# A two-layer attention and feed-forward kernel: stage order set anew with GpSimd's measured durations, one copied column less, unread matmuls in planned idle times

## The chip, the cores and the metric

The kernel runs on one core of one Trainium2 chip, as one program. The metric is the device time in microseconds (us). A core has five engines with a queue each: TensorE (PE, matmuls, with the loading of weights shown apart as PEld), VectorE (DVE), ScalarE (ACT), GpSimd (POOL) and SyncE (SP, which here issues nearly all DMAs). Each engine executes its own queue in order, and waits for other engines by semaphores.

## The reference

Four blocks are applied to x (2048 rows of 512), attention, feed-forward, attention, feed-forward, each as x + block(layernorm(x)). All of it is fp32.

```python
# attention, 32 heads of 16, 4 segments of 512 rows; M and z start at 0
for s in range(N):
    logits = einsum("bhqd,bhkd->bhqk", qs, ks) * scale + mask
    a_dot = einsum("bhqk,bhkd->bhqd", softmax(logits), vs)
    num = einsum("bhld,bhde->bhle", phi(qs), M)
    den = einsum("bhld,bhd->bhl", phi(qs), z)[..., None] + 1e-6
    outs.append(g * num / den + (1.0 - g) * a_dot)
    M = M + einsum("bhld,bhle->bhde", phi(ks), vs)
    z = z + einsum("bhld->bhd", phi(ks))
# then the heads are put together and multiplied by wo
# feed-forward, 1792 inner columns
(silu(x @ w_gate) * (x @ w_up)) @ w_down
```

## The kernel before

**Numbers.** An fp32 operand is split into a rounded high part (written by ACT, or by POOL in L492) and a rest (high subtracted again, by DVE or POOL). Three one-pass matmuls, high by high, rest by high and high by rest, take the place of one fp32 matmul.

**Attention.** A layer has 32 units (4 segments, 4 groups of heads, 2 halves). `qk_proj` projects q and k of a group (L295, the helper of all projections), ACT copies the result (L491), POOL splits it (L492, L494), and SP writes it to memory and reads it back in another layout (`load3`, tiles cq and ck, cleared beforehand by POOL in L522 to L525). `mx_units` takes row maxima (PE L558, DVE L564, transposed by PE in L573, then written by an ACT DMA), `at_units` makes the exponentials (PE L609, ACT L615, POOL's causal mask L619), multiplies with v (L636) and normalises on DVE. `mem_read` and `mem_update` (L690, L706, L718) carry the memory M, z. `wo_proj` ends a segment. Layernorm statistics run on DVE and POOL (L367 to L379), and the normalised rows are transposed by PE against the identity matrix `ident` (L387), which DVE and POOL make at the start (L319, L320).

**Feed-forward.** The inner 1792 columns are 7 chunks of 256, the 2048 rows 4 blocks of 512, taken as two pairs (m = 0 and 1). Chunk 0 is computed plainly (`up`, L1017). Chunks 1 to 6 use a scheme with seven products for a pair of row blocks (`strassen`, L1047, sums on DVE in L1060). It needs sums of row blocks, the four T tiles, made once per pair by `make_t` (sums L961, high part on ACT L982, rest on DVE L983), and sums of weight blocks, made for each chunk by `load_s`: two raw loads, four sums on POOL (L900), then high parts on ACT (L913) and rests on POOL (L914). `gate` and `finish` apply silu and the product (L998 to L1004), `down` multiplies with w_down and adds to the residual on DVE (L1091, L1096). `load_d` loads w_down's part, with the rests on POOL (L867).

**The order of the work.** No order is written out by hand. The program first records every operation with an engine, an assumed cost, its dependences and a priority, which is a due time: `at(v)` sets it to a base plus v times a stage length. The constants `PRE` (start of a layer), `OFF` (steps of an attention unit), `EP` (chunk 0), `PAIR`, `STEP`, `WAT`, `TAT`, `FIN` and `WQ1` are such due times. Then `issue` simulates all engines: whenever an engine is free, it takes the operation of lowest due time among those that are ready, and that order is the order of the engine's queue in the program. It also gives out the 8 PSUM banks (tag "ps"). Assumed costs matter only through this order. POOL's are written as numbers at each call of `gp`.

**The copied column.** `pool_turn` (L918) makes POOL copy one column of a tile. Operations that are made to depend on this copy come behind it in POOL's queue, so they start only when that tile has been written. Ahead of a chunk c > 1 the tile is the second one of the chunk before's gated product; ahead of chunk 1 of the second pair it is the T tile TT[2], whose rests DVE writes. The up weights of the chunk, the gate weights of the next one and w_down's part wait for it.

Of the kernel before, what the change touches and what calls it, by code (L numbers as in the profile page):

```python
# [12 lines left out]
OP = mybir.AluOpType  # L13
# [11 lines left out]
NB = 3  # L25
CAP = {'pj': 3, 'plt': 3, 'pmx': 3, 'ppv': 3, 'ff': 6, 'st': 6}
LPW = 3
WOT = ("st", "st", "pj", "pj")
EARLY_AT = (23, 25, 26)
PAIR, STEP, WAT, TAT = 11.852, 7.441, 15.217, (16.363, 16.627)  # L30
T3E = "dve"
FIN = 4.95
WQ1 = -11.849
TA, TF = 15.0, 16.7
OFF = ({'qe': (-8.094, 0.816), 'at': (3.287, 3.306), 'mx': (-0.131, -0.724), 'lf': (1.377, -12.744), 'mr': (-1.477, 8.495), 'mu': (-0.96, 1.713), 'wo': (1.48, 1.471), 'qk': (-3.167, 5.871), 'v': (3.082, -3.254), 'lp': (-0.438, 1.332)},
       {'qe': (-13.863, -20.735), 'at': (1.287, 1.907), 'mx': (0.952, -1.245), 'lf': (-8.163, -17.558), 'mr': (12.428, -6.81), 'mu': (-3.524, 1.251), 'wo': (0.699, 4.133), 'qk': (2.417, 0.184), 'v': (-2.402, 1.541), 'lp': (-15.902, 3.529)})
PRE = {'w1': -7.923, 'w2': -0.782, 'w3': 1.908, 'c': -7.288, 'mb': 12.995, 'lv': 2.037, 'lo': 1.091, 'gate': 1.265, 'v': 1.734, 'dv': 17.818, 'qk1': -29.691, 'mx': -0.352}
EP = {'w': 7.501, 'wn': 13.81, 'ln': -3.176, 'dn': -0.03, 'up': -1.79}
POOL_W = ""
TABLE = 1.28  # L40
DRAIN = {("full", "cols"): 0.097, ("cols", "full"): 0.147}
# [38 lines left out]
class Program:  # L80
# [70 lines left out]
    def issue(self):  # L151
# [102 lines left out]
def infini_swiglu(ctx: ExitStack, tc: tile.TileContext, x, wq, wk, wv, wo, beta, wg, wu, wd, out,  # L254
# [33 lines left out]
    def gp(cost, fn, reads, writes):  # L288
        op("pool", cost, fn, reads, writes)
# [75 lines left out]
    def ln_norm(xt, view, xk, tags, on_act=False):  # L365
        st, mv, rs = sb("bst", [128, 6], ring=4), sb("bmv", [128, 2], ring=4), sb("brs", [128, 2], ring=4)
        dve(512, lambda: nc.vector.bn_stats(out=st.ap, in_=view(xt.ap)), [(xt, xk)], [st])  # L367
        dve(8, lambda: nc.vector.bn_aggr(out=mv.ap, in_=st.ap), [st], [mv])
        gp(0.18, lambda: nc.gpsimd.tensor_scalar_add(mv.ap[:, 1:2], mv.ap[:, 1:2], EPS), [mv], [mv])
        gp(0.46, lambda: nc.gpsimd.tensor_tensor(out=rs.ap[:, 0:1], in0=mv.ap[:, 1:2], in1=mhalf.ap, op=OP.pow),  # L370
           [mv, mhalf], [rs])
        dve(4, lambda: nc.vector.scalar_tensor_tensor(out=rs.ap[:, 1:2], in0=mv.ap[:, 0:1], scalar=-1.0,
                                                      in1=rs.ap[:, 0:1], op0=OP.mult, op1=OP.mult), [mv, rs], [rs])
        xn = sb(tags, [128, 512])
        if on_act:
            act(512, lambda: nc.scalar.activation(xn.ap, view(xt.ap), AF.Identity, scale=rs.ap[:, 0:1],
                                                  bias=rs.ap[:, 1:2]), [(xt, xk), rs], [xn], sbuf=True)
            return xn
        gp(0.75, lambda: nc.gpsimd.tensor_scalar(out=xn.ap, in0=view(xt.ap), scalar1=rs.ap[:, 0:1],  # L379
                                                 scalar2=rs.ap[:, 1:2], op0=OP.mult, op1=OP.add),  # L380
           [(xt, xk), rs], [xn])
        return xn
# [27 lines left out]
    def attention(lay, x_in, x_out, slots, T, hook):  # L410
# [70 lines left out]
        def qk_proj(s, n, nm, tag="pj"):  # L481
            g = GRP.setdefault((s, n), {})
            if "nat" not in NAT:
# [5 lines left out]
                lambda kc: n, lambda kc: None, "b")  # L489
            raw = sb("raw", [128, 512])  # L490
            act(512, lambda: nc.scalar.copy(raw.ap, ps.ap), [ps], [raw])  # L491
            gp(0.59, lambda: nc.gpsimd.tensor_scalar(out=nat.ap[:, a, 0, :], in0=raw.ap, scalar1=1.0, scalar2=0.0,  # L492
                                                     op0=OP.mult, op1=OP.add), [raw], [(nat, (a, 0))])
            gp(1.23, lambda: nc.gpsimd.tensor_sub(nat.ap[:, a, 1, :], raw.ap, nat.ap[:, a, 0, :].bitcast(F32)),  # L494
               [raw, (nat, (a, 0))], [(nat, (a, 1))])
            if (nm == "q" and s > 0) or (nm == "k" and s < NSEG - 1):
                ph = sb(f"phik_{n - 2}" if s == nseg - 1 and n > 1 else f"phi{nm}_{n % 2}", [128, 512])
# [87 lines left out]
        def at_units(u):  # L585
# [16 lines left out]
            def lt(kt, qt):  # L602
                def f():
# [12 lines left out]
                        view().rearrange("p x i c -> p (x i c)"), ps.ap, AF.Exp, scale=SCALE), [ps], [(Pb, key)],  # L616
                        table="exp")
                    if kt == qt:
                        gp(0.593, lambda: nc.gpsimd.affine_select(  # L619
                            out=view()[:, 0], in_=view()[:, 0], pattern=[[0, 4], [1, 128]], compare_op=OP.is_ge,  # L620
                            fill=0.0, base=0, channel_multiplier=-1), [(Pb, key)], [(Pb, key)])
                return f
# [25 lines left out]
            def post():  # L648
# [10 lines left out]
                if h == 1:  # L659
# [14 lines left out]
                    gp(1.23, lambda: nc.gpsimd.tensor_sub(tl.ap[:, n, :], of.ap, th.ap[:, n, :].bitcast(F32)),  # L674
                       [of, (th, n)], [(tl, n)])

            units = [lt(0, q) for q in range(4)] + [lt(1, q) for q in (1, 2, 3)]
# [169 lines left out]
    def ffn(base, x_in, x_out, slots, T):  # L847
# [40 lines left out]
        def load_s(c, nm, after=()):  # L888
# [8 lines left out]
            S1, S2, S3, S4 = [lambda i=i, o=o: m[i].ap[:, o] for i, o in ((0, 1), (0, 0), (1, 0), (1, 1))]  # L897

            def ew(f, out, x, y, reads, w_):
                gp(0.65, lambda: getattr(nc.gpsimd, f)(out(), x(), y()), reads, [w_])  # L900
# [5 lines left out]
            for wt, o0, o1, src, read in ((a, 0, 1, lambda: v0()[:, :, 0:128].rearrange("p k (o f) -> p o k f", o=1), r0),  # L906
                                          (a, 1, 3, lambda: m[0].ap, m[0]),
                                          (b, 0, 2, lambda: v1().rearrange("p k (o f) -> p o k f", o=2), r1),
                                          (b, 2, 4, lambda: m[1].ap, m[1])):
                n = 256 * (o1 - o0)  # L910
                hi = lambda wt=wt, o0=o0, o1=o1: wt.ap[:, o0:o1, 0]
                lo = lambda wt=wt, o0=o0, o1=o1: wt.ap[:, o0:o1, 1]
                act(n, lambda hi=hi, src=src: nc.scalar.copy(hi(), src()), [read], [(wt, (o0, 0))], sbuf=True)  # L913
                gp(n / 400, lambda hi=hi, lo=lo, src=src: nc.gpsimd.tensor_sub(lo(), src(), hi().bitcast(F32)),  # L914
                   [read, (wt, (o0, 0))], [(wt, (o0, 1))])
                P.ops[-1].deps |= set(after)

# [211 lines left out]
        for m in range(2):  # L1129
# [24 lines left out]
            for c in range(1, NF):  # L1154
# [93 lines left out]
```

## Time and profile before

| | us |
|---|---|
| median of 3 runs | 1881.71 |
| lowest and highest | 1880.82, 1883.06 |
| the profiled execution | 1878.99 |
| its span, first to last instruction | 1877.2 |
| its mean granted TensorE clock | 0.995 |

In rows of the profile, L12 is line 12 of the kernel before. A row of the view by windows gives the stretch, its length, the busy time and the number of instructions of PE, PEld, DVE, ACT and POOL, the share of TensorE's full clock that was granted (PEclk), the DMA share and GB/s. A row of the view of waits gives who waited for whom, the total in us, how often, and the longest. A row of the timeline gives start and duration in us, engine, line, operation, output and inputs, how many instructions were merged, and in brackets the engine's idle time before it and what ended it. A row of a group gives the count, busy time in us and mean duration in ns.

### The profile page before, as it was taken

The page shows a single profiled execution, that of the slowest core. Times are in us where ns is not written, and L with a number is a line of the kernel's source. Part 1 is how long each engine was busy: PE and PEld are TensorE (multiplying, and loading weights), DVE is VectorE, ACT ScalarE, POOL GpSimd, SP SyncE. Part 2 cuts the span into 40 slices and gives each one's busy share as a digit, 9 for nine tenths or more (in the row PEclk, how much of TensorE's full clock was granted, in tenths as well). Part 3 has the DMA queues.
Part 4 walks back from the last instruction along what each step waited for, and adds up shares of the span by engine and source line. Part 5 has one row for each costly group of instructions (what it writes and reads, how often), then busy time and mean ns, then how long its engine had stood idle before and what let it go on. Part 6 is the DMA issues. An engine that isn't in the chain of part 4 may idle for free.

```text
span 1877.2 us, 33021 instructions
## 1 busy us (share of the span) xinstructions
PE 1825.3 (97%) x11360; PEld 1450.6 (77%) x11360; DVE 1407.5 (75%) x3834; ACT 873.1 (47%) x1629; POOL 918.9 (49%) x1186
## 2 busy tenths in 40 slices
PE   7999999999999999999989999999999999999999
PEld 5787787877778887788867877778777788878887
DVE  6878788778876678766776777787898766796656
ACT  4565564555533432433345655556454433333432
POOL 6344444444655654647533444444446647445551
PEclk9999999999999999999999999999999999999999
DMA  7535444464232132111373353455642311312121
GB/s 236 148 102 147 135 133 144 144 214 119 74 119 61 46 91 89 52 50 57 114 217 101 106 163 115 130 167 140 188 124 74 123 51 56 94 64 57 44 58 45
DMA packets 126967, 206.14 MB, mean 110 GB/s; under 512 B 14160, under 2 KB 52048, under 8 KB 126800
## 3 DMA queue, kind: packets, MB, share of 16 engines
q1 hardware_dynamic: 124752, 203.49, 36.7%
q8 instruction: 91, 1.49, 0.3%
q10 hardware_dynamic: 2048, 0.53, 0.1%
q14 instruction: 76, 0.62, 0.1%
HBM read 136.34 MB, written 67.11 MB: 108 GB/s over the span
## 4 chain that ended last, share of the span: by engine, by line
PE 48%; DVE 7%; issue 2%; DMA 2%; POOL 1%; ACT 1%; SPq 0%; DVEq 0%; POOLq 0%; ACTq 0%
PE ps L1047 18%; PE ps L1091 10%; PE ps L295 7%; PE ps L636 3%; PE ps L558 3%; PE ps L609 3%; DVE junk L564 2%; DMA s<-nm 1%; PE ps L1017 1%; DVE tt L961 1%; DVE s L983 1%; DVE s L1096 1%; PE ps L387 1%; DVE mx L564 0%; DVE of L961 0%
## 5 line engine op out<-in xcount | busy, mean ns | idle before, releaser
L1047 PE MATMUL ps<-s,s 128*128 128x512 f32 x2016 | 547.3, 396 | 9.5 <-ACT s L982 4.6
L295 PE MATMUL ps<-s,s 128*128 128x512 f32 x1536 | 526.2, 407 | 2.7 <-ACT s L451 1.2
L564 DVE CUSTOM_DVE_ANT_0 junk<-ps,amask 128x128 bf16<-128x128 f32 (+3 forms) x1024 | 433.5, 484 | 46.5 <-PE ps L558 45.1
L1047 PEld LDWEIGHTS ps<-s,s 128*128 128x128 f32 x2016 | 376.7, 188 | 106.0 <-ACT s L982 6.7
L1091 PE MATMUL ps<-s,vt 128*128 128x512 f32 x1296 | 378.0, 397 | 2.2 <-ACT vt L1003 2.2
L295 PEld LDWEIGHTS ps<-s,s 128*128 128x128 f32 x1536 | 287.2, 191 | 51.6 <-issue 6.1
L615 ACT ACTIVATE s<-ps 128x512 f32<-128x512 f32 x448 | 253.9, 609 | 108.5 <-PE ps L609 97.2
L1091 PEld LDWEIGHTS ps<-s,vt 128*128 128x128 f32 x1296 | 245.2, 189 | 58.6 <-ACT vt L1003 2.6
L558 PE MATMUL ps<-ck,s 127*128 127x256 f32 (+2 forms) x1024 | 276.6, 334 | 5.7 <-DMA ck<-scrk 4.9
L609 PE MATMUL ps<-s,ck 128*128 128x256 f32 x1280 | 250.6, 287 | 6.4 <-DMA s<-nm 4.5
L609 PEld LDWEIGHTS ps<-s,ck 128*128 128x128 f32 x1280 | 221.3, 189 | 38.3 <-issue 4.9
L1096 DVE TENSOR_TENSOR s<-s,ps 128x512 f32<-128x512 f32 x224 | 150.1, 683 | 92.0 <-PE ps L1091 91.7
L619 POOL TENSOR_SCALAR_AFFINE_SELECT s<-s 128x512 f32<-128x512 f32 x192 | 126.8, 663 | 171.9 <-ACT s L615 166.6
L558 PEld LDWEIGHTS ps<-ck,s 127*128 127x128 f32 x1024 | 177.6, 189 | 28.8 <-issue 6.4
L914 POOL TENSOR_TENSOR s<-mem,s 128x512 fp32r<-128x512 f32 x96 | 130.7, 1362 | 0.0
L492 POOL TENSOR_SCALAR s<-raw 128x512 fp32r<-128x512 f32 x64 | 45.4, 709 | 173.9 <-ACT raw L491 163.6
L1017 PE MATMUL ps<-s,s 128*128 128x512 f32 x384 | 123.9, 400 | 0.9 <-ACT s L391 0.9
L921 POOL COPY turn<-vt 128x1 f32<-128x1 f32 x20 | 3.7, 186 | 235.6 <-DVE vt L1004 235.6
L636 PE MATMUL ps<-s,vt 128*32 128x384 f32 (+3 forms) x1536 | 115.7, 419 | 0.1
L636 PEld LDWEIGHTS ps<-s,vt 128*32 128x32 f32 x1536 | 43.3, 109 | 64.1 <-issue 46.2
L615 ACT ACTIVATE pc<-ps 128x512 f32<-128x512 f32 x128 | 78.7, 615 | 19.9 <-PE ps L609 19.3
L494 POOL TENSOR_TENSOR s<-raw,s 128x512 fp32r<-128x512 f32 x64 | 84.3, 1317 | 4.3
(172 smaller groups left out, 2585.3 us busy)
## 6 DMA issues: line engine op xcount, KB each, us to landing
s<-scrq SPq DMA_DIRECT2D x128, 192.0 KB, 3.5
ck<-scrk SPq DMA_DIRECT2D x128, 192.0 KB, 4.5
scrq<-s SPq DMA_DIRECT2D x32, 512.0 KB, 3.6
scrk<-s SPq DMA_DIRECT2D x32, 512.0 KB, 3.3
scrq<-s SPq DMA_DIRECT2D x32, 256.0 KB, 3.2
scrk<-s SPq DMA_DIRECT2D x32, 256.0 KB, 2.5
s<-xmid SPq DMA_DIRECT2D x32, 256.0 KB, 5.2
xin<-xmid SPq DMA_DIRECT2D x32, 256.0 KB, 2.7
```

Source lines behind the costliest of these rows:

```text
L295: pe(n, passes, lambda: nc.tensor.matmul(view(ps.ap), lhsT=av(a.ap), rhs=bv(b.ap), start=start, stop=stop), [(a, rk[0]), (b, rk[1])], [ps])
L558: nc.tensor.matmul(ps.ap[:, a * 256:a * 256 + nk], lhsT=cq.ap[0:127, 2 * j + p, qt * 128:(qt + 1) * 128], rhs=ck.ap[0:127, p, 0:nk], start ...
L564: dve(w, lambda a=a, qt=qt, w=w, ps=ps, junk=junks[qt % 2]: nc.vector.tensor_tensor_reduce(out=junk.ap[:, :w], in0=ps.ap[:, a * 256:a * 25 ...
L609: nc.tensor.matmul(ps.ap[:, 256 * p:256 * p + 256], lhsT=ck.ap[:, p, kt * 128:kt * 128 + 128], rhs=cq.ap.rearrange("r (j p) c -> r p j c", ...
L615: act(512, lambda: nc.scalar.activation(view().rearrange("p x i c -> p (x i c)"), ps.ap, AF.Exp, scale=SCALE), [ps], [(Pb, key)], table="exp")
L619: gp(0.593, lambda: nc.gpsimd.affine_select(out=view()[:, 0], in_=view()[:, 0], pattern=[[0, 4], [1, 128]], compare_op=OP.is_ge, fill=0.0, ...
L636: nc.tensor.matmul(ps.ap[32 * i:32 * i + 32, qt * 128:(qt + k) * 128], lhsT=vt.ap[:, kt, VW * hd:VW * hd + 32], rhs=view(k=k)[:, :, idx], ...
L914: gp(n / 400, lambda hi=hi, lo=lo, src=src: nc.gpsimd.tensor_sub(lo(), src(), hi().bitcast(F32)), [read, (wt, (o0, 0))], [(wt, (o0, 1))])
L1017: pe(512, 1, lambda i=i, j=j, kc=kc, x=x, ps=ps, wt=wt: nc.tensor.matmul(ps.ap, lhsT=wt.ap[:, i, kc, cs], rhs=XT[b][j].ap[:, :, kc], start ...
L1047: pe(512, 1, lambda i=i, kc=kc, x=x, buf=buf, view=view: nc.tensor.matmul(ps.ap, lhsT=w.ap[:, o, i, kc], rhs=view(buf.ap, kc), start=(x == 0),
L1091: pe(512, 1, lambda i=i, j=j, fi=fi, x=x, ps=ps, wt=wt, cs=cs: nc.tensor.matmul(ps.ap, lhsT=ht.ap[:, 0:2048].rearrange("p (f a c) -> p f a ...
L1096: dve(512, lambda ps=ps, t=t: nc.vector.tensor_add(xb.ap[:, t, :], xb.ap[:, t, :], ps.ap), [ps, (xb, t)], [(xb, t)])
```

## The change

Three things change, and no matmul of the computation is added or removed.

1. Assumed costs of POOL's operations are raised, and all due times are set anew.
2. The copied column ahead of chunk 1 of the second pair is left out (before, only the first pair had none).
3. `issue` puts runs of unread matmuls into PE's queue. Where the simulated PE is idle for over 0.8 us, and a PSUM bank is free since before that idle time, it emits as many matmuls of 128 columns as fit at 0.215 us each, less 0.35 us, at most 16. They multiply half of `ident` by itself in fp32, into the bank that came free last, and nothing reads the result. The simulation itself takes no account of them. For the first run PE counts as idle from 3.5 us on.

```diff
+WARM = (0.8, 0.35, 16)
...
-PAIR, STEP, WAT, TAT = 11.852, 7.441, 15.217, (16.363, 16.627)
+PAIR, STEP, WAT, TAT = 11.353, 1.597, 1.08, (12.624, 17.012)
...
-FIN = 4.95
-WQ1 = -11.849
+FIN = -2.787
+WQ1 = -3.055
...
-PRE = {'w1': -7.923, 'w2': -0.782, 'w3': 1.908, 'c': -7.288, 'mb': 12.995, 'lv': 2.037, 'lo': 1.091, 'gate': 1.265, 'v': 1.734, 'dv': 17.818, 'qk1': -29.691, 'mx': -0.352}
-EP = {'w': 7.501, 'wn': 13.81, 'ln': -3.176, 'dn': -0.03, 'up': -1.79}
+PRE = {'w1': -7.357, 'w2': -1.301, 'w3': 4.634, 'c': 6.066, 'mb': 18.459, 'lv': 4.718, 'lo': -0.662, 'gate': 1.688, 'v': 9.33, 'dv': 18.454, 'qk1': -33.774, 'mx': -8.469}
+EP = {'w': -0.609, 'wn': 14.483, 'ln': -1.109, 'dn': -5.448, 'up': -16.361}
...
-        done, bus, table, mode = 0, 0.0, "exp", "full"
+        done, bus, table, mode, idle = 0, 0.0, "exp", "full", 3.5
...
+            if e == "pe":
+                spare = max([fr for fr in free["ps"] if fr[0] <= idle], default=None)
+                beats = min(WARM[2], int((start - idle - WARM[1]) / 0.215)) if start - idle > WARM[0] else 0
+                if spare and beats:
+                    self.warm(spare[1], beats)
...
+            if e == "pe":
+                idle = t[e]
...
+    def warm(slot, beats):
+
+        t = psum.tile([128, 512], F32, name=f"ps_{slot}", tag=f"ps_{slot}")
+        for _ in range(beats):
+            nc.tensor.matmul(t[:, 0:128], lhsT=ident.ap[0:64], rhs=ident.ap[0:64], start=True, stop=True)
+    P.warm = warm
...
-                elif m == 0:
+                else:
                     turn = []
-                else:
-                    turn = pool_turn(lambda t=TT[2]: t.ap[:, 1, 3, 1, 127:128], (TT[2], (1, 1)))
```

All ten entries of `OFF` change for both layers in the same manner (least those of maxima and exponentials, by at most 1.3 units of 15 us, most those of layernorm, by up to 17.7). POOL's assumed costs change like this:

| operation | line | before, us | after, us |
|---|---|---|---|
| power in layernorm | L370 | 0.46 | 0.60 |
| normalise 512 columns | L379 | 0.75 | 0.85 |
| high part of q, k | L492 | 0.59 | 0.70 |
| rest of q, k; of the attention's output | L494, L674 | 1.23 | 1.32 |
| causal mask | L619 | 0.593 | 0.66 |
| sum of weight blocks | L900 | 0.65 | 0.85 |
| rest of n weight columns | L914 | n / 400 | 0.3 + n / 480 |

More of the change, by code (lines that the diff above doesn't have):

```diff
@@ L369, in ln_norm @@
         gp(0.18, lambda: nc.gpsimd.tensor_scalar_add(mv.ap[:, 1:2], mv.ap[:, 1:2], EPS), [mv], [mv])
-        gp(0.46, lambda: nc.gpsimd.tensor_tensor(out=rs.ap[:, 0:1], in0=mv.ap[:, 1:2], in1=mhalf.ap, op=OP.pow),
+        gp(0.6, lambda: nc.gpsimd.tensor_tensor(out=rs.ap[:, 0:1], in0=mv.ap[:, 1:2], in1=mhalf.ap, op=OP.pow),
            [mv, mhalf], [rs])
@@ L378, in ln_norm @@
             return xn
-        gp(0.75, lambda: nc.gpsimd.tensor_scalar(out=xn.ap, in0=view(xt.ap), scalar1=rs.ap[:, 0:1],
+        gp(0.85, lambda: nc.gpsimd.tensor_scalar(out=xn.ap, in0=view(xt.ap), scalar1=rs.ap[:, 0:1],
                                                  scalar2=rs.ap[:, 1:2], op0=OP.mult, op1=OP.add),
@@ L491, in qk_proj @@
             act(512, lambda: nc.scalar.copy(raw.ap, ps.ap), [ps], [raw])
-            gp(0.59, lambda: nc.gpsimd.tensor_scalar(out=nat.ap[:, a, 0, :], in0=raw.ap, scalar1=1.0, scalar2=0.0,
+            gp(0.70, lambda: nc.gpsimd.tensor_scalar(out=nat.ap[:, a, 0, :], in0=raw.ap, scalar1=1.0, scalar2=0.0,
                                                      op0=OP.mult, op1=OP.add), [raw], [(nat, (a, 0))])
-            gp(1.23, lambda: nc.gpsimd.tensor_sub(nat.ap[:, a, 1, :], raw.ap, nat.ap[:, a, 0, :].bitcast(F32)),
+            gp(1.32, lambda: nc.gpsimd.tensor_sub(nat.ap[:, a, 1, :], raw.ap, nat.ap[:, a, 0, :].bitcast(F32)),
                [raw, (nat, (a, 0))], [(nat, (a, 1))])
@@ L618, in f @@
                     if kt == qt:
-                        gp(0.593, lambda: nc.gpsimd.affine_select(
+                        gp(0.66, lambda: nc.gpsimd.affine_select(
                             out=view()[:, 0], in_=view()[:, 0], pattern=[[0, 4], [1, 128]], compare_op=OP.is_ge,
@@ L673, in post @@
                     act(512, lambda: nc.scalar.copy(th.ap[:, n, :], of.ap), [of], [(th, n)], sbuf=True)
-                    gp(1.23, lambda: nc.gpsimd.tensor_sub(tl.ap[:, n, :], of.ap, th.ap[:, n, :].bitcast(F32)),
+                    gp(1.32, lambda: nc.gpsimd.tensor_sub(tl.ap[:, n, :], of.ap, th.ap[:, n, :].bitcast(F32)),
                        [of, (th, n)], [(tl, n)])
@@ L899, in ew @@
             def ew(f, out, x, y, reads, w_):
-                gp(0.65, lambda: getattr(nc.gpsimd, f)(out(), x(), y()), reads, [w_])
+                gp(0.85, lambda: getattr(nc.gpsimd, f)(out(), x(), y()), reads, [w_])
                 P.ops[-1].deps |= set(after)
@@ L913, in load_s @@
                 act(n, lambda hi=hi, src=src: nc.scalar.copy(hi(), src()), [read], [(wt, (o0, 0))], sbuf=True)
-                gp(n / 400, lambda hi=hi, lo=lo, src=src: nc.gpsimd.tensor_sub(lo(), src(), hi().bitcast(F32)),
+                gp(0.3 + n / 480, lambda hi=hi, lo=lo, src=src: nc.gpsimd.tensor_sub(lo(), src(), hi().bitcast(F32)),
                    [read, (wt, (o0, 0))], [(wt, (o0, 1))])
```

4 lines of the change are left out of this document (2 added, 2 removed).

## The prediction

> **What bounds the kernel now.** I read the page's head first, then the busy times by stage, then what TensorE (PE) waited for, then the timeline where it waited longest.
>
> ```profile
> span 1877.2 us, 33021 instructions
> ...
> PE 1825.3 (97%) x11360; PEld 1450.6 (77%) x11360; DVE 1407.5 (75%) x3834; ACT 873.1 (47%) x1629; POOL 918.9 (49%) x1186
> ```
>
> PE is busy for 1825.3 of 1877.2 us, and the change removes no useful matmul. So a gain has to come out of the 51.9 us in which PE is idle, or out of matmuls that run slowly. By stage:
>
> ```profile
> core 0: us, PE busy (x) PEld busy (x) DVE busy (x) ACT busy (x) POOL busy (x), PEclk, DMA share, GB/s
> 0.00:60.00 60.00, 43.43 (x192) 34.55 (x193) 39.90 (x131) 27.69 (x50) 31.55 (x54) 0.97 0.73 220
> 60.00:440.00 380.00, 377.25 (x3175) 301.16 (x3174) 298.50 (x1141) 215.04 (x425) 165.44 (x249) 1.00 0.49 145
> 440.00:720.00 280.00, 275.74 (x1386) 216.42 (x1386) 213.06 (x420) 117.42 (x211) 157.96 (x187) 1.00 0.27 81
> 720.00:760.00 40.00, 35.71 (x149) 27.89 (x148) 37.41 (x63) 12.94 (x24) 23.10 (x24) 0.91 0.29 92
> 760.00:900.00 140.00, 140.00 (x606) 113.27 (x605) 89.74 (x137) 54.36 (x95) 78.38 (x85) 1.00 0.19 55
> 900.00:1000.00 100.00, 91.84 (x444) 73.77 (x446) 76.37 (x215) 40.27 (x73) 43.12 (x51) 1.00 0.52 156
> 1000.00:1400.00 400.00, 393.46 (x3331) 310.99 (x3323) 311.02 (x1190) 223.64 (x440) 172.30 (x264) 1.00 0.50 141
> 1400.00:1640.00 240.00, 237.66 (x1109) 188.19 (x1108) 175.89 (x291) 100.38 (x176) 138.97 (x161) 1.00 0.26 78
> 1640.00:1700.00 60.00, 56.74 (x245) 44.92 (x244) 51.99 (x79) 22.84 (x40) 28.14 (x28) 0.97 0.21 71
> 1700.00:1877.00 177.00, 173.44 (x748) 139.46 (x746) 113.62 (x174) 58.47 (x101) 79.89 (x88) 1.00 0.16 50
> ```
>
> The chunks of the feed-forward part are full: 760 to 900 has no idle PE and 606 matmuls in 140 us, 0.231 us each. No order is faster there. Idle PE time lies in six places: 16.6 us at the start, 2.8 and 6.5 in the two attention stages (60 to 440, 1000 to 1400), 4.3 in 720 to 760 and 3.3 in 1640 to 1700 (each the change to the second pair of row blocks), 8.2 around the change of layers, and 3.6 at the end. What ended the waits:
>
> ```profile
> PE ps L387 <- ACT xn L376: 9.8, 1, 9.8
> PE ps L558 <- DMA ck<-scrk: 4.9, 4, 2.8
> PE ps L573 <- DVE mx L564: 4.7, 9, 1.7
> PE ps L1047 <- ACT s L982: 4.6, 4, 2.6
> ...
> PE ps L1047 <- POOL s L914: 4.2, 2, 3.1
> PE ps L706 <- DVE phik L501: 3.0, 1, 3.0
> ```
>
> The first wait of 9.8 us and the last 3.6 us no order of matmuls takes away. Beside idle time there are stretches at half clock (column PEclk):
>
> ```profile
> 20.00:40.00 20.00, 16.98 (x68) 12.52 (x67) 10.30 (x19) 7.61 (x13) 12.10 (x20) 0.91 0.90 273
> 740.00:760.00 20.00, 16.15 (x58) 12.11 (x57) 18.27 (x28) 6.25 (x13) 14.99 (x14) 0.83 0.10 26
> 1200.00:1220.00 20.00, 18.50 (x113) 14.13 (x112) 12.59 (x42) 10.93 (x21) 8.16 (x10) 0.91 0.49 139
> 1680.00:1700.00 20.00, 17.59 (x69) 13.69 (x70) 14.24 (x19) 7.99 (x14) 15.27 (x14) 0.91 0.22 67
> ```
>
> They cost 20 x (0.09 + 0.17 + 0.09 + 0.09) = 8.8 us in all, behind waits. So about 51.9 - 9.8 - 3.6 + 8.8 = 47 us is the most that better order and warmth could ever give; a few of them are in reach.
>
> **The copied column.** Only the second pair of row blocks has it ahead of chunk 1, once a layer:
>
> ```profile
> 746.44 1.18 POOL L921 COPY turn<-s 128x1 f32<-128x1 f32 x1 [3.87 <-DVE s L983]
> 751.76 0.73 PE L1047 MATMUL ps<-s,s 128*128 128x512 f32 x1 [3.15 <-POOL s L914]
> 1675.07 0.58 POOL L921 COPY turn<-s 128x1 f32<-128x1 f32 x1 [18.05 <-DVE s L983]
> 1682.15 0.50 PE L1047 MATMUL ps<-s,s 128*128 128x512 f32 x1 [2.56 <-ACT s L982]
> ```
>
> GpSimd (POOL) stands in this copy for 3.87 and 18.05 us until VectorE (DVE) has written the last part of one T tile; behind it in POOL's queue are the sums and splits of chunk 1's up weights, and PE at 751.76 waits 3.15 us for just such a split (L914). Without the copy the four sums (L900) can run at once; the splits still need the old weights' place. In the first layer the copy and its wait leave, so L914 ends several us earlier and the 3.15 us go; next late is the T tile (L982), and it is fed by DVE. There is a price, which DVE's rows before and behind the copy show:
>
> ```profile
> L961 DVE TENSOR_TENSOR tt<-s,s 128x512 f32<-128x512 f32 x4 | 2.6, 681 | 0.0
> ...
> L961 DVE TENSOR_TENSOR of<-of,s 128x512 f32<-128x512 f32 x1 | 1.2, 1219 | 0.0
> ```
>
> While POOL is silent (1660 to 1675) an addition of the T chain takes 0.681 us; beside POOL's sums 1.219, which is 0.54 more. Four sums laid beside the chain delay it by up to 4 x 0.54 = 2.2 us, but the same 2.2 us are then missing behind. First layer: 3.15 us of wait and 20 x 0.17 = 3.4 us of half clock, less 2.2: between -6.6 (all saved) and +2.2; I take -4, since the wait hangs on L914 alone. Second layer: 2.56 us and 1.8 us of half clock hang on the DVE chain itself, which gets no shorter; between -4.4 and +2.2, and I take -1.5.
>
> **The start.** In the second row POOL clears tiles ahead of making ident; the change moves these memsets back in priority.
>
> ```profile
> 0.79 0.95 POOL L522 MEMSET s<- 128x1024 f32 x1 [0.29 <-POOLq L1235]
> ...
> 3.55 0.29 POOL L320 TENSOR_SCALAR_AFFINE_SELECT ident<-ident 128x128 f32<-128x128 f32 x1
> ...
> 28.70 0.45 PE L706 MATMUL ps<-ident,phik 128*128 128x128 f32 x1 [3.02 <-DVE phik L501]
> ...
> L387 PE MATMUL ps<-ident,xn 128*128 128x128 f32 x16 | 3.8, 428 | 9.8 <-ACT xn L376 9.8
> L295 PE MATMUL ps<-s,s 128*128 128x512 f32 x8 | 3.6, 626 | 1.2 <-ACT s L451 1.2
> ...
> L295 PE MATMUL ps<-s,s 128*128 128x512 f32 x30 | 7.8, 406 | 0.0
> ```
>
> The first 8 matmuls of L295 take 3.6 us, 0.45 each, the next 30 take 7.8, 0.26 each: PE starts at half speed. The planned idle time ahead of the first transposes surely asks for a full run of 16 unread matmuls, and they need nothing but ident, ready at 3.84 us here and earlier if it comes ahead of two memsets. What one costs is bounded by the nearest fp32 rows:
>
> ```profile
> 1200.59 0.86 PE L690 MATMUL ps<-mb,phiq 128*128 128x136 f32 x6
> ```
>
> Six records, 0.28 us the last of them, so some 0.116 from start to start; the page's L690 calls stand as two records each, which makes one unread matmul about 0.22 us, or 0.44 cold, and 16 of them 3.5 to 7 us. That fits ahead of 9.8 us, so the run is free. If PE is then at full speed, 8 x 0.19 = 1.5 us go from the first projection, and about as much from the 16 transposes, of which the casts behind them hide a part. At 28.70 the 3.02 us wait and the 1.8 us of half clock are a place that a plan can foresee too. Between 0 and -5; I take -2. By the Trainium skill (TensorE: Matmul & The Clock Gate, "What's actually happening") the array starts at half rate and gets the full one after about 3.4 us of sustained work. By that rule the run ends warm and the start gives its whole 3 us; the trace agrees in so far as 3.8 us of transposes with a gap behind them were not enough.
>
> **The new costs and order.** The new constants come closer to the profile:
>
> ```profile
> L914 POOL TENSOR_TENSOR s<-mem,s 128x512 fp32r<-128x512 f32 x96 | 130.7, 1362 | 0.0
> ...
> L492 POOL TENSOR_SCALAR s<-raw 128x512 fp32r<-128x512 f32 x64 | 45.4, 709 | 173.9 <-ACT raw L491 163.6 <-issue 8.6 <-POOL mb L729 0.8
> ```
>
> A split measures 1.362 us where the planner counted 512/400 = 1.28 and now counts 1.37; the copy of L492 measures 0.709, 0.59 before, 0.70 now. POOL is busy under half of either attention stage, so 0.1 us an instruction matters only where its result is awaited: in 900 to 1000, where PE waits on ck, which goes POOL split, write to memory, read back. I give that place -1.5 (from -5, the ck waits, to +5, as much again). In the attention stages all queues are reordered, ACT's, DVE's, POOL's and SP's DMAs too; idle time there is 9.3 us, so -9 to +9, and I take -0.5, since nothing says which way. In the full chunk stages the moved steps (finish first, chunks closer together) have nothing to gain.
>
> **Unread runs elsewhere.** They stand in PE's queue wherever the plan had over 0.8 us idle; every matmul behind waits for them. Where the chip idles at the same place they cost nothing; where it does not, up to 16 x 0.22 = 3.5 us each. They also write the bank that came free last, so PE first waits for that bank's reader on ACT or DVE, if it runs later than planned. I put +1 (0 to +13). They cannot help at 751, 1203 and 1683 if the plan saw no idle time there.
>
> **Sum.** -4 - 1.5 - 2 - 1.5 - 0.5 + 1 = -8.5 us. The profiled execution took 1878.99 us, 1.8 more than its span and 2.7 less than the median of 1881.71; it would become 1870.5, the median 1873.2.
>
> **The rivals.** A difference under 0.2%, 3.8 us, cannot be told from none here.
> (1) The waits only move: PE's waits are many and short, and a new order makes new ones of its own, since no plan has the 0.54 us of the DVE and POOL collision in it. For it: 9 waits of L573 on DVE that no constant here names. Then only the start's 2 us are left: 1880, 0.19.
> (2) Slower by unread runs: places of planned idle time drift, and the runs delay ready matmuls in the attention and layer-change stages. It decides once more than 12 us of runs, say seven of half length (8 x 0.22 each), meet a busy queue: 1873.2 + 13 = 1886. Against it: stage changes, where idle time is, stay where they are. 0.10.
> (3) Slower by the port: POOL's sums and four splits, freed, all lie beside the T chain, 8 x 0.54 = 4.3 us a layer, in stages where DVE is already busy 37.4 of 40 and 52.0 of 60 us, and PE falls to half clock behind each wait as now. It decides if DVE has no idle time left ahead of the chain. None of the 5.5 us is saved, the other terms (-2 - 1.5 - 0.5 + 1 = -3) stay, 8.6 are lost: 1881.7 - 3 + 8.6 = 1887, 0.11. The Trainium skill (SBUF — State Buffer, "Who interferes with whom") says the same: a VectorE instruction with two SBUF inputs contends with a GpSimd one that reads SBUF. The 0.681 and 1.219 us agree.
> (4) The runs do not do what they say: they leave the clock as it is, so the start's 2 us stay lost and the rest holds: 1875.2, 0.10 (0.07 of it faster).
>
> **The numbers.** The forecast has 0.50. Faster: 0.50 + 0.07 = 0.57; same: 0.19 + 0.03 = 0.22; slower: 0.10 + 0.11 = 0.21. The range goes down by the better ends of the first layer's copy, the start and the layer change (2.6 + 3 + 3.5, to 1864) and up to rivals 2 and 3 (1887). Faster cases alone: 1864 to 1878.
>
> **What would show it.** Right: no row of L921 with a long wait ahead of chunk 1, no PE wait on L914 near 750, PEclk there above 0.83; the first 8 matmuls of L295 at about 0.4 us instead of 0.626; more than 11360 matmuls, two records for each unread one, most of them in PE's old idle time; less than 51.9 us idle beside them. Wrong: L961 at 1.2 us over the whole T chain and DVE without a gap there; unread runs directly behind and ahead of busy matmuls whose inputs were long ready; new PE waits in 60 to 440 or 1000 to 1400 that add up to more than 9.3 us.

## The result, and the profile after

The changed kernel takes 1894.32 us (median of 5 runs, 1890.01 to 1896.15), the kernel before 1881.71 (5 runs, 1876.40 to 1883.96). The ratio is 1.0067, interval 1.0046 to 1.0087: slower by two thirds of a per cent. The forecast was 1873.2, the range ended at 1887. The profiled execution took 1895.1 us. A run far off the others of its kernel is in no ratio; there is one, of the six of before_new_costs below, which took 3688.06 us, and no trace says why.

Lines below L26 have moved in the changed kernel: projections are L303 (L295 before), transposes L402 (L387), maxima L573 and L579 (L558, L564), their transposes L588 (L573), logits for the exponentials L624 (L609), products with v L651 (L636), high parts of T on ACT L997 (L982) and their rests on DVE L998 (L983), products of the seven-product scheme L1062 (L1047). L319 is the unread matmul. The head of the page:

```profile
span 1893.4 us, 33298 instructions
PE 1850.9 (98%) x11530; PEld 1474.9 (78%) x11530; DVE 1409.3 (74%) x3834; ACT 869.6 (46%) x1625; POOL 919.7 (49%) x1184
```

The unread matmuls alone, as a group:

```profile
L319 PE MATMUL ps<-ident 64*128 64x128 f32 x170 | 27.8, 326 | 2.1 <-POOL ident L335 2.1
```

PE is idle for 42.5 us, less than the 51.9 before. But 27.8 us of the busy time are unread work. Without it PE is busy for 1850.9 - 27.8 = 1823.1 us, 2.2 less than before, and it does nothing useful for 1893.4 - 1823.1 = 70.3 us, 18.4 more. So the useful matmuls did not get slower; they came later. By stage (stretch, length, busy time and count of PE, PEld, DVE, ACT and POOL, granted clock, DMA share, GB/s):

```profile
0.00:60.00 60.00, 56.31 (x270) 47.98 (x271) 38.63 (x124) 27.04 (x49) 31.35 (x54) 1.00 0.72 214
60.00:440.00 380.00, 377.20 (x3160) 299.40 (x3159) 295.74 (x1135) 213.87 (x419) 161.57 (x245) 1.00 0.49 145
440.00:720.00 280.00, 273.45 (x1392) 215.61 (x1391) 213.35 (x426) 117.39 (x214) 162.55 (x190) 1.00 0.28 81
720.00:760.00 40.00, 34.03 (x152) 27.36 (x151) 36.23 (x61) 12.89 (x23) 22.48 (x27) 0.95 0.33 104
900.00:1000.00 100.00, 98.53 (x480) 79.66 (x479) 78.58 (x215) 40.32 (x73) 46.86 (x52) 1.00 0.53 161
1000.00:1400.00 400.00, 389.82 (x3277) 308.67 (x3276) 305.42 (x1164) 224.74 (x433) 169.36 (x257) 0.99 0.48 140
1640.00:1700.00 60.00, 55.73 (x255) 44.31 (x253) 55.02 (x84) 22.16 (x40) 30.39 (x34) 1.00 0.26 84
```

The first stretch shows how a busy share deceives: PE is busy for 56.31 us, 12.9 more than before, and yet behind in its work, since 84 of the 270 records are unread (an unread matmul stands as two records). The stages of the second pair (720 to 760, 1640 to 1700) are less full than before (35.71 and 56.74). The second attention stage (1000 to 1400) has 3.6 us less of busy PE. What ended PE's longest waits:

```profile
PE ps L1062 <- ACT s L997: 11.2, 5, 6.0
PE ps L624 <- DMA s<-nm: 6.5, 6, 2.3
PE ps L573 <- DVE mx L579: 2.6, 5, 1.1
PE ps L1062 <- DVE tt L1075: 2.4, 3, 0.8
PE ps L319 <- POOL ident L335: 2.1, 1, 2.1
```

The wait for POOL's split (4.2 us before) is off the list; the one for the T tiles' high parts on ACT has grown from 4.6 to 11.2.

Which stage loses can be read by laying the two traces on each other: give each useful matmul its usual time from start to start, sum these up, and compare when each trace reached the same sum. Changed minus before, the lag is +2.2 us at 73 us, +0.9 at 469, +4.0 at 549, +5.9 at 782, +6.3 at 882, +4.6 at 1018, +0.6 at 1363, and then +11.4 at 1446, +12.9 at 1674, +14.3 at 1829 and +16.1 at the end. Most of the loss falls in some 80 us, at the end of the second layer's attention. The two orders differ, so a single one of these figures moves by 2 to 4 us with the place where it is read; the step between 1363 and 1446 is larger than that.

### The profile page after: what moved, and what is told of

It is laid out like the page before. It is cut to its first block, busy times and chain, and to the rows that moved or that the text cites. A ratio compares the mean times of both kernels' runs of the same rounds, so it can differ in the third digit from the quotient of the medians.

```text
span 1893.4 us, 33298 instructions
## 1 busy us (share of the span) xinstructions
PE 1850.9 (98%) x11530; PEld 1474.9 (78%) x11530; DVE 1409.3 (74%) x3834; ACT 869.6 (46%) x1625; POOL 919.7 (49%) x1184
## 4 chain that ended last, share of the span: by engine, by line
PE 48%; DVE 7%; issue 2%; DMA 2%; ACT 1%; POOL 1%; SPq 0%; DVEq 0%; ACTq 0%
PE ps L1062 17%; PE ps L1106 11%; PE ps L303 8%; PE ps L573 3%; PE ps L624 3%; PE ps L651 3%; PE ps L1032 2%; DMA s<-nm 1%; DVE junk L579 1%; DVE tt L976 1%; DVE vt L1019 1%; PE ps L402 1%; DVE s L998 0%; DVE s L1111 0%; DVE xn L976 0%
## 5 line engine op out<-in xcount | busy, mean ns | idle before, releaser
L1062 PE MATMUL ps<-s,s 128*128 128x512 f32 x2016 | 548.3, 397 | 18.0 <-ACT s L997 11.2
L303 PE MATMUL ps<-s,s 128*128 128x512 f32 x1536 | 522.6, 406 | 0.1
L1062 PEld LDWEIGHTS ps<-s,s 128*128 128x128 f32 x2016 | 376.8, 188 | 117.0 <-ACT s L997 13.4
L579 DVE CUSTOM_DVE_ANT_0 junk<-ps,amask 128x128 bf16<-128x128 f32 (+3 forms) x1024 | 434.4, 482 | 43.5 <-PE ps L573 42.7
L303 PEld LDWEIGHTS ps<-s,s 128*128 128x128 f32 x1536 | 287.0, 190 | 46.3 <-issue 4.5
L573 PE MATMUL ps<-ck,s 127*128 127x256 f32 (+2 forms) x1024 | 278.5, 335 | 5.2 <-DVE mx L579 2.6
L624 PE MATMUL ps<-s,ck 128*128 128x256 f32 x1280 | 244.8, 288 | 7.9 <-DMA s<-nm 6.5
L624 PEld LDWEIGHTS ps<-s,ck 128*128 128x128 f32 x1280 | 217.7, 190 | 37.3 <-DVE r L669 5.0
L573 PEld LDWEIGHTS ps<-ck,s 127*128 127x128 f32 x1024 | 178.1, 190 | 31.2 <-issue 6.0
L651 PE MATMUL ps<-s,vt 128*32 128x384 f32 (+3 forms) x1536 | 115.7, 419 | 0.1
L651 PEld LDWEIGHTS ps<-s,vt 128*32 128x32 f32 x1536 | 43.5, 109 | 64.4 <-issue 48.2
```

Source lines behind the costliest of these rows:

```text
L303: pe(n, passes, lambda: nc.tensor.matmul(view(ps.ap), lhsT=av(a.ap), rhs=bv(b.ap), start=start, stop=stop), [(a, rk[0]), (b, rk[1])], [ps])
L573: nc.tensor.matmul(ps.ap[:, a * 256:a * 256 + nk], lhsT=cq.ap[0:127, 2 * j + p, qt * 128:(qt + 1) * 128], rhs=ck.ap[0:127, p, 0:nk], start ...
L579: dve(w, lambda a=a, qt=qt, w=w, ps=ps, junk=junks[qt % 2]: nc.vector.tensor_tensor_reduce(out=junk.ap[:, :w], in0=ps.ap[:, a * 256:a * 25 ...
L624: nc.tensor.matmul(ps.ap[:, 256 * p:256 * p + 256], lhsT=ck.ap[:, p, kt * 128:kt * 128 + 128], rhs=cq.ap.rearrange("r (j p) c -> r p j c", ...
L651: nc.tensor.matmul(ps.ap[32 * i:32 * i + 32, qt * 128:(qt + k) * 128], lhsT=vt.ap[:, kt, VW * hd:VW * hd + 32], rhs=view(k=k)[:, :, idx], ...
L1062: pe(512, 1, lambda i=i, kc=kc, x=x, buf=buf, view=view: nc.tensor.matmul(ps.ap, lhsT=w.ap[:, o, i, kc], rhs=view(buf.ap, kc), start=(x == 0),
```

## The experiments

No kernel here leaves part of the computation out; unread matmuls, where a kernel has them, are extra work. Each is compared with the kernel before on the same chip. 0.1% is 1.9 us.

**Which of the three parts.** R says that the unread runs cost the time, O that the new costs and due times do by themselves, P that POOL's freed work collides with DVE once the copied column is gone.

```diff
# after_no_runs: the changed kernel without unread matmuls
-WARM = (0.8, 0.35, 16)
+WARM = (1e9, 0.35, 16)
# before_with_runs: the kernel before, with the changed one's WARM and warm()
# after_with_copy: the changed kernel with the copied column
-                else:
+                elif m == 0:
                     turn = []
+                else:
+                    turn = pool_turn(lambda t=TT[2]: t.ap[:, 1, 3, 1, 127:128], (TT[2], (1, 1)))
# before_without_copy: the kernel before with turn = [] there
```

after_no_runs: 

> The changed kernel without its 85 unread matmuls; the order of everything else is the same. Theory R (the runs cost the time: they start where the plan saw idle time and the work behind them is ready): the second run at the start holds the first projection from 14.7 to 18.4 us, the third one holds the second projection by some 2 us, those from 1412 to 1436 cost about 3.5, the short ones 0.44 each; so 6 to 10 us less than the changed kernel, 1884 to 1888. Theory O (the new order is slower by itself): within 3 us of the changed kernel, 1891 to 1896. Theory P (DVE and POOL collide once the copy is gone): as theory O.

Measured: 1.0050 (1.0035 to 1.0065).

before_with_runs: 

> The kernel before with unread matmuls in its own plan's idle times, and nothing else. Theory R: slower than before by 4 to 9 us (1886 to 1891), with the first projection held to 18 us or so. Theory O and P: within 3 us of before. If the runs did what they are meant for, the first 8 matmuls of the first projection would take 0.23 us from start to start and the time would be 1 to 3 us shorter.

Measured: 1.0011 (1.0002 to 1.0021).

after_with_copy: 

> The changed kernel with the copied column ahead of chunk 1 of the second pair put back. Theory P: 4 to 8 us less than the changed kernel. Theory R and O: within 3 us of it, since the stage of the second pair shows only 2 us of new loss in each layer.

Measured: 1.0052 (1.0032 to 1.0071).

before_without_copy: 

> The kernel before without the copied column ahead of chunk 1 of the second pair, and nothing else. The prediction's reasoning: 3 to 8 us less than before, the 3.15 us wait of PE on the weights' rest (L914) gone. Theory P: 4 to 9 us more than before. If the copy is neutral: within 2 us.

Measured: 1.0005 (0.9995 to 1.0016).

The runs are worth 0.0017 one way (1.0067 against 1.0050) and 0.0011 the other; the copied column 0.0015 and 0.0005. The first figures compare intervals that overlap, so their size is rough, and before_without_copy has 1 in its interval, as the branch "neutral" of its expectation says. But neither part shows a gain on either base, and neither carries the loss. What is left has to be the order:

```diff
# after_order_only: both other parts taken back; only costs and due times are new
-WARM = (0.8, 0.35, 16)
+WARM = (1e9, 0.35, 16)
# and the copied column as in after_with_copy
```

> The changed kernel with the copied column put back and without unread matmuls: what is left is the new costs with the new due times. If the three parts add up (runs 0.0017, copy 0.0015 of the 1.0067): ratio 1.003 to 1.004, some 6 to 7 us. If the order alone is harmless and the two others need each other: 0.999 to 1.001. If it carries everything: 1.005 or more.

Measured: 1.0042 (1.0026 to 1.0058). So some 0.42 of the 0.67% are the order's (O), and the other two parts together make up the rest, about as the first branch of the expectation has it. Its trace is ahead of the kernel before by 2.9 us at 73 us and by 9.0 at 1362, and behind by 1.5 at 1445: 10.5 us go there, and 2.8 more between 1597 and 1647 leave it 5.3 behind at the end. The stretch from 1360 to 1460 in the kernel before, in the changed one and in after_order_only:

```profile
1360.00:1460.00 100.00, 96.17 (x647) 73.29 (x647) 85.70 (x251) 49.21 (x91) 52.67 (x75) 1.00 0.38 108
```

```profile
1360.00:1460.00 100.00, 93.61 (x664) 73.55 (x663) 80.97 (x266) 48.21 (x92) 52.77 (x76) 0.97 0.36 104
```

```profile
1360.00:1460.00 100.00, 91.38 (x598) 70.75 (x599) 78.74 (x236) 45.95 (x87) 50.70 (x73) 0.97 0.29 83
```

```profile
PE ps L588 <- DVE mx L579: 3.2, 2, 2.8
PE ps L624 <- DMA s<-nm: 2.6, 1, 2.6
PE ps L624 <- DVE r L669: 1.9, 1, 1.9
```

The last fence is what PE waited for there in after_order_only: row maxima, their way through memory, and a normalisation that frees a bank. All are steps of attention units. PE runs out of other work while their chain passes through DVE, and falls to half clock on top (0.97). The changed kernel meets the same place with 34 of its 664 records unread, and waits there for the same maxima on their way through memory:

```profile
PE ps L624 <- DMA s<-nm: 4.4, 2, 2.3
```

**Why the new order is behind.** E says that the new `EP` brings chunk 0's work too early, so that it is missing beside the last units. D says that it is other constants. Each base has no unread runs.

```diff
# no_runs_old_ep: after_no_runs with EP of before
# no_runs_old_off1: after_no_runs with the second layer's OFF of before
# no_runs_old_costs: after_no_runs with POOL's costs of before
# before_new_costs: the kernel before with the changed one's POOL costs, e.g.
-            gp(0.59, lambda: nc.gpsimd.tensor_scalar(out=nat.ap[:, a, 0, :], in0=raw.ap, ...
+            gp(0.70, lambda: nc.gpsimd.tensor_scalar(out=nat.ap[:, a, 0, :], in0=raw.ap, ...
```

no_runs_old_ep: 

> The changed kernel without unread matmuls and with the five due times EP of the kernel before (chunk 0 of the feed-forward part, whose layernorm is then due 2.1 x 16.7 = 35 us earlier, ahead of the end of attention). Theory E (the new EP lets PE run out of chunk-0 work at the end of layer 1's attention, so its waits on DVE's row maxima lie bare): the 9 us lost between 1362 and 1445 come back, ratio to before 0.999 to 1.002, and L1032 starts near 1395. Theory D (the loss is spread over the whole order, or sits in layer 1's attention constants): ratio stays at 1.004 to 1.006.

Measured: 1.0089 (1.0074 to 1.0104).

no_runs_old_off1: 

> The changed kernel without unread matmuls and with layer 1's ten attention offsets (second half of OFF) of the kernel before. Theory E: 1.004 to 1.006 as without this edit, with the waits of L588 and L624 on L579 near 1390 to 1410 still there. Theory D, in the form that layer 1's attention order is to blame: 0.999 to 1.002.

Measured: 1.0154 (1.0140 to 1.0167).

no_runs_old_costs: 

> The changed kernel without unread matmuls, all new due times kept, POOL's assumed costs as before. If the due times carry the loss, 1.004 to 1.006; if the new costs carry it, 0.999 to 1.002; due times that were found with one set of costs may also fit another one badly, then above 1.006.

Measured: 1.0268 (1.0251 to 1.0284).

before_new_costs: 

> The kernel before with the new assumed costs of POOL alone. The prediction's reasoning: measured durations are a better plan, 0.996 to 1.000. Theory E: within 0.2% of before, as its due times still bring chunk 0 early. If the new costs by themselves spoil the order: 1.003 or more.

Measured: 1.0203 (1.0188 to 1.0218).

E falls: with the old `EP` the kernel is slower, and by the same reckoning of lag 6 to 8 us still go between 1363 and 1445. The old offsets of the second layer make it slower still, which neither E nor D had foreseen. My expectation of the last kernel falls hard too: costs nearer to the profile made the old order 2% slower. All four mixtures of old and new are slower than either whole. So a set of due times seems to go with the costs that it stands with; how either set was found is not on record.

**Are measured costs worse, or any others?** C says that the measured costs make a worse plan, so harm grows with the change. F says that the old due times are fitted to the old costs, so that any neighbouring plan is behind, whichever way it lies.

```diff
# before_one_cost: 64 calls of L492
-            gp(0.59, lambda: nc.gpsimd.tensor_scalar(...
+            gp(0.70, lambda: nc.gpsimd.tensor_scalar(...
# before_cost_hair: the same line, 0.59 -> 0.60
# before_cost_mask: the 256 causal masks of L619, 0.593 -> 0.66
# before_due_shift: costs kept, the first layer's exponentials 1.5 us later
-OFF = ({'qe': (-8.094, 0.816), 'at': (3.287, 3.306), ...
+OFF = ({'qe': (-8.094, 0.816), 'at': (3.387, 3.406), ...
```

before_one_cost: 

> The kernel before with one assumed cost changed, that of L492 (0.59 to its measured 0.70 us, 64 calls), all due times kept. If the loss of 2.0% with all eight new costs grows with their size: 1.001 to 1.004. If any change of a cost throws the order into another one of no special quality: 1.005 to 1.02. If a measured cost is better: below 1.000.

Measured: 1.0142 (1.0128 to 1.0155).

before_cost_hair: 

> The kernel before with L492's assumed cost 0.60 in place of 0.59 us. Theory C (measured costs make a worse order, in proportion): 0.01 of the 0.11 us that cost 1.4%, so within 0.2% of before. Theory F (a fitted optimum; any other order is behind): 1.003 to 1.02.

Measured: 1.0105 (1.0087 to 1.0123).

before_cost_mask: 

> The kernel before with the assumed cost of the causal mask alone changed, 0.593 to its measured 0.66 us (256 calls). Theory C: about 1.01, as 0.07 us on four times as many calls as L492. Theory F: 1.003 to 1.02, with no relation to size.

Measured: 1.0177 (1.0155 to 1.0199).

before_due_shift: 

> The kernel before with all costs kept and layer 0's two due times of the attention units (at) later by 0.1 of 15 us. Theory C: within 0.2% of before, since no cost changes. Theory F: 1.002 to 1.02.

Measured: 1.0059 (1.0040 to 1.0079).

F holds for these four neighbours, C does not. Eleven times the change of cost (0.11 against 0.01 us) costs 1.4 times as much, and a due time moved with all costs kept costs 0.59%. A hundredth of a microsecond in 64 of POOL's operations can delay nothing by itself: 64 x 0.01 is 0.6 us, and the loss is 20. It changes which operation the simulation takes, and with that everything behind: PE's matmuls in before_cost_hair follow the kernel before for 97 records of 11360, to about 40 us, those in before_due_shift for 2808, to about 367 us. No cost was moved away from its measured value, so that this harms as well is argued from the shift of the due time and not shown. Where such an order loses can be seen from 490 to 580, in the first layer's chunk stage: the kernel before, before_cost_hair, and before_due_shift with PE's waits there.

```profile
490.00:580.00 90.00, 87.77 (x376) 69.23 (x375) 71.64 (x104) 30.87 (x55) 51.27 (x51) 1.00 0.31 100
```

```profile
490.00:580.00 90.00, 84.68 (x410) 64.41 (x410) 68.05 (x104) 35.59 (x64) 48.16 (x54) 0.96 0.30 94
```

```profile
490.00:580.00 90.00, 82.42 (x377) 63.86 (x376) 67.94 (x98) 32.89 (x58) 47.87 (x52) 0.98 0.28 92
```

```profile
PE ps L295 <- DVE raw L1001: 2.8, 1, 2.8
PE ps L1047 <- DVE xn L1060: 2.1, 1, 2.1
```

In the kernel before these two waits are 0.2 us each.

**What the unread matmuls do to the clock.** A says that any sustained work of PE raises the clock, B that small fp32 work does not. The times at which the clock becomes full are those of the traces' clock records; the column of granted clock counts only from the first of these records on, which is why it shows 1.00 for the changed kernel's first 60 us. The first two kernels put only the run ahead of the first transposes into the kernel before, with taller or wider matmuls; the third makes all the changed kernel's runs taller.

```diff
# before_first_run_full: 128 rows in place of 64, first run only
-            nc.tensor.matmul(t[:, 0:128], lhsT=ident.ap[0:64], rhs=ident.ap[0:64], start=True, stop=True)
+            nc.tensor.matmul(t[:, 0:128], lhsT=ident.ap, rhs=ident.ap, start=True, stop=True)
# before_first_run_bf16: first run only, nearly all its data zeros
+            nc.tensor.matmul(t, lhsT=amask.ap[:, 384:512], rhs=amask.ap, start=True, stop=True)
# after_runs_full: the changed kernel, every run over 128 rows
```

before_first_run_full: 

> The kernel before with the first run alone, 16 unread matmuls ahead of the first transposes, over all 128 rows of the identity matrix where the change took 64. Theory A (the clock follows any sustained PE work): with 7 us of work from 3.9 us on the full clock is granted by 11 us at the latest, the first 8 matmuls of L295 take 0.23 us each, and the time is 0 to 3 us less than before. Theory B (such unread work of small fp32 matmuls on few columns does not count, or too little): the full clock still comes only 3 to 5 us after the transposes begin, 13 to 18 us, and the time is within 0.1% of before, or 1 us more since the run ends after the transposes' input is ready.

Measured: 0.9995 (0.9986 to 1.0005).

before_first_run_bf16: 

> The same place and number, but each unread matmul is one bf16 pass of 512 columns over 128 rows (the mask tile, nearly all zeros, times itself), 0.43 us each at half clock. Theory A: full clock by 11 us. Theory B in the form that only small fp32 matmuls count too little: full clock by 11 us here and not in the other run. If the data count (zeros move nothing): not here either.

Measured: 0.9993 (0.9984 to 1.0002).

after_runs_full: 

> The changed kernel with its unread matmuls over all 128 rows. If the runs cost time because they leave the clock cold: full clock by 7 us, the second run at the start half as long, 1.003 to 1.005, as without runs or a little less. If they cost it by where they stand: 1.006 to 1.007 as the changed kernel.

Measured: 1.0072 (1.0055 to 1.0089).

The granted clock in the traces becomes full at 17.99 us in the kernel before, at 15.8 in before_with_runs and at 22.3 in the changed kernel, which have 7.2 us of 64-row runs from 3.90 and 2.13 on. In after_with_copy, with the changed kernel's runs, it is full at 12.9, and the eleven other kernels without any run lie between 12.3 and 19.6. With 128 rows it is full at 7.03, with bf16 at 6.82, and in after_runs_full at 8.2. So neither theory holds as it was put: A falls for 64 rows, B for the same fp32 matmuls over 128. The runs as they were written are not the work that raises the clock. Whether it is the rows or the amount of data was not tried. The start of the changed kernel, PE and the cast of the first weights on ACT:

```profile
2.13 7.19 PE L319 MATMUL ps<-ident 64*128 64x128 f32 x32 [2.13 <-POOL ident L335]
9.81 3.68 PE L402 MATMUL ps<-ident,xn 128*128 128x128 f32 x16 [0.49 <-ACT xn L391]
13.41 5.06 PE L319 MATMUL ps<-ident 64*128 64x128 f32 x22
14.00 4.26 ACT L466 CAST s<-s 128x512 fp32r<-128x512 f32 x8
18.40 4.82 PE L303 MATMUL ps<-s,s 128*128 128x512 f32 x12
23.16 3.61 PE L319 MATMUL ps<-ident 64*128 64x128 f32 x30
```

The first of these casts is done at about 14.6 (4.26 us for eight), but the second run of 22 records stands ahead of the first projection until 18.40, at half clock; the third stands between the first and the second projection. The same rows of after_runs_full and, behind them, of before_first_run_full:

```profile
12.30 2.62 PE L319 MATMUL ps<-ident 128*128 128x128 f32 x22
14.68 3.04 PE L303 MATMUL ps<-s,s 128*128 128x512 f32 x12
17.55 3.51 PE L319 MATMUL ps<-ident 128*128 128x128 f32 x30
20.82 6.32 PE L303 MATMUL ps<-s,s 128*128 128x512 f32 x26
```

```profile
3.90 5.31 PE L319 MATMUL ps<-ident 128*128 128x128 f32 x32 [3.90 <-POOL ident L335]
10.29 2.15 PE L402 MATMUL ps<-ident,xn 128*128 128x128 f32 x12 [1.08 <-ACT xn L391]
14.79 5.85 PE L303 MATMUL ps<-s,s 128*128 128x512 f32 x24 [1.19 <-ACT s L466]
22.51 5.27 PE L303 MATMUL ps<-s,s 128*128 128x512 f32 x13 [1.88 <-ACT s L466]
```

Runs over 128 rows bring the first projection forward from 18.40 to 14.68 us (14.73 in the kernel before, without runs), and the whole kernel is still no faster than the changed one, 1.0072 against 1.0067. That speaks for the places where the runs stand, not for the cold clock, as what they cost. With the first run alone and a warm PE, projections wait for the casts (1.19 and 1.88 us) in place of the clock: the start hangs on ACT's casts of weights, and the casts of the second wait, from 20.29 us on, in turn on the weights' DMA. A warm start is worth nothing that these runs can show; the better of the two, 0.9993, has 1 in its interval.

**The copied column, locally.** PE's waits from 715 to 790 in before_without_copy, then POOL and DVE at that place in its timeline:

```profile
PE ps L1091 <- DVE s L1096: 3.9, 1, 3.9
PE ps L1047 <- ACT s L982: 2.5, 1, 2.5
```

```profile
744.92 1.82 POOL L914 TENSOR_TENSOR s<-mem,s 128x512 fp32r<-128x512 f32 x1
745.50 1.78 DVE L961 TENSOR_TENSOR xn<-xn,xn 128x512 f32<-128x512 f32 x1
747.85 1.74 POOL L914 TENSOR_TENSOR s<-phik,s 128x512 fp32r<-128x512 f32 x1
750.07 1.76 DVE L983 TENSOR_TENSOR s<-xn,s 128x512 fp32r<-128x512 f32 x1
754.74 2.07 PE L1091 MATMUL ps<-s,vt 128*128 128x512 f32 x4 [3.93 <-DVE s L1096]
```

The wait of 3.1 us on L914 is gone as planned. But POOL's splits now run beside the T chain: an addition of L961 takes 1.78 us where 0.681 is its mean alone, and PE waits once for DVE's addition to the residual (3.9 us) and once for a T tile's high part on ACT, which comes from that chain (2.5). In the changed kernel the T tile's high part alone costs 6.0 us there, in after_with_copy 2.3:

```profile
PE ps L1062 <- ACT s L997: 6.0, 1, 6.0
```

```profile
PE ps L1062 <- ACT s L997: 2.3, 1, 2.3
```

This is rival 3's mechanism, at its place. Its size is not the 5.5 us of gain lost and 8.6 more, but a net one us on the kernel before, which cannot be told from none, and three on the changed one, since the wait that was removed is real as well.

## Why the prediction was wrong, step by step

- **The new costs and order (-1.5 and -0.5): the step that failed.** It said that the new constants come closer to the profile, that a cost matters only where its result is awaited, and that of the attention stages "nothing says which way". Measured, the order alone is +0.42%, 7.9 us, of the 12.6 between the medians. That lies inside the prediction's own bounds (-9 to +9 and -5 to +5): the middle was wrong, put near zero as if either way were as likely. The old order behaves like one fitted to its costs: every neighbour that was run is slower, costs nearer to the truth with the old due times by 2.0%, a hair's change by 1.05%. With its own due times the new plan wins most of that back and lands behind. The layer change gave about what was predicted (the lag falls by 1.7 us from 882 to 1018, and the waits on ck between 900 and 1000 from 4.3 us to 2.8 in after_no_runs); the end of the second layer's attention, to which the sum gave no term of its own, takes 10.8 in the changed kernel, unread runs included. The list of idle places also left out the 4.3 us of 440 to 720 and the 2.3 of 1400 to 1640, where the sum saw nothing to gain; an order can still lose there, as the lag from 469 to 549 shows. Which due time makes the last units of the second layer lose between 1363 and 1446 is open.
- **The copied column (-4 and -1.5).** The wait on L914 left as said. The step "since the wait hangs on L914 alone" was wrong: the next waits, on DVE and ACT, were as long (3.9 and 2.5 us in before_without_copy, for 3.1). Measured between +0.0005 and +0.0015, 1 to 3 us of loss, the smaller one not clear of none.
- **The start (-2).** In the changed kernel the first run did fit ahead of the first transposes and cost nothing there (it ends at 9.32 us, they begin at 9.81); in before_with_runs, where it starts at 3.90, they begin at 11.03 in place of 9.78. The runs do not raise the clock (rival 4's reason), and where a raised clock was forced it gained nothing. By the Trainium skill (TensorE: Matmul & The Clock Gate, "What's actually happening") 7.2 us of sustained work should have ended at full rate; the traces agree for runs over 128 rows (full 3.1 us after their start in one kernel, 6.1 in the other), not for those over 64.
- **Unread runs elsewhere (+1).** Start included, the runs cost 0.0011 to 0.0017, 2 to 3 us, where -2 and +1 had been put. The places are those of rival 2: directly ahead of projections at 13.41 and 23.16, and 34 records from 1360 to 1460. Its price of 13 us was too high (and its sum counts the +1 twice: 1885, not 1886). In the two profiled executions, 9.9 of the 27.8 us of unread work add to the time without useful work (70.3 us against 1885.1 - 1824.7 = 60.4 in after_no_runs), more than the 3 us by the ratios, and the rest fell where PE would have been idle.
- **The rivals.** Rival 1 had the right reason ("a new order makes new ones of its own") and set its price at zero, on the assumption that one order is as good as another. That is where the chance of slower was lost: all five neighbours of the old order that were run are slower, so a neighbour was no fair draw. From the forecast -8.5 to the measured +12.6 us, some 10 are the order's, 6.5 to 8.5 the copied column's and 3 to 4 those of the start and the runs.
- **What would show it.** As listed for right: no wait on L914, PEclk of 0.90 from 740 to 760, more than 11360 matmuls, less idle PE; only the first projection's matmuls stayed slow, 0.638 us in the mean from 18.3 to 22.1. As listed for wrong: waits in the second attention stage, unread runs ahead of ready matmuls, DVE slowed over the T chain. Most of the first list was met and the kernel was slower: idle time that is filled with unread work says nothing.

## What to carry to other kernels

Where a simulation with assumed costs writes the order and due times go with them, take the pair as one: any single cost that is changed, even towards its measured value, must be expected to cost time (1.05 to 1.77% here, a due time 0.59%) until the due times are found again on the chip. A wait that is removed is worth only its distance to the next one behind it, so price the next one before booking the gain. And count useful work, not busy time, when filler is added: PE went from 97 to 98% busy while doing its work later.

## What the runs showed of the hardware

- Sixteen unread fp32 matmuls over 64 rows, 7.2 us of PE without a gap, left it at half clock (full at 22.3, 15.8 and 12.9 us in the three kernels with them, 12.3 to 19.6 in the twelve without any run), and in the changed kernel the next 22 records too; the same over 128 rows gave full clock 3.1 us after their start (6.1 in another kernel), and 16 bf16 matmuls of 512 columns, whose data are nearly all zeros, after 2.7. So data that are nearly all zeros do not keep the clock down.
- Stretches at half clock between two at full clock last 3.413 us, 6.827 or 10.240, one, two or three times as much, in the clock records of all 18 profiles.
